# An attention block's row maxima transposed in SBUF, and two down projections of each block held for the next

## The chip, the cores and the metric

The kernel is one program on one NeuronCore of a Trainium2 chip. Its time is the device time in microseconds of one execution. Five engines run side by side, each through its own list of instructions in order: PE (TensorE, matrix products into PSUM), DVE (VectorE), ACT (ScalarE), POOL (GpSimd, which here works on SBUF only) and SP, whose list holds the DMA issues. PEld in a profile is PE's weight load, which can lie beside its matmuls. Engines wait for each other by semaphores.

## The reference

Shapes: one sequence of 2048 rows of width 512; 32 query heads of 16 columns share one key and one value head; a gated feed-forward of width 1792.

```python
mod = (silu(c) @ w_mod)                     # sa, ca, ga, sb, cb, gb: rows of 512
h = layernorm(x) * (1 + ca) + sa
q, k, v = h @ wq, h @ wk, h @ wv            # q: 32 heads of 16; k, v: one head of 16
p = softmax(q k^T / 4)                      # per head, over 2048 keys
x = x + ga * ((p v, heads side by side) @ wo)
h = layernorm(x) * (1 + cb) + sb
x = x + gb * (((h @ w_gate) * (h @ w_up)) @ w_down)
```

All in float32. The kernel splits operands of most products into a float16 high part and a float16 low part, and adds three products for one (terms high-high, low-high, high-low); p v is done in float32.

## The kernel before, in words

The sequence is cut into NB = 4 blocks of 512 rows, and each block's 32 heads into 8 groups of four: 32 units u = 8 b + g. A unit takes 32 **steps**; step s = 32 u + i. A step does one key tile for half of the unit: `qk_exp` makes two score tiles of 128x512 (L487, tile sc) which ACT exponentiates into P (L600), and `pv` multiplies earlier P tiles with the values (L612). There are 1024 steps and 2048 exponentials, so two exponentials in a trace are one step.

The exponent needs the maximum of each row of scores first. It is found by a second, earlier pass over the same scores: `max_mm` makes a 128x512 tile (L487, tile mx) and DVE reduces it to one column (L564, mpart). This pass runs LEAD = 38 steps ahead of the main one, two reduces a step; the first 38 steps of it are a loop of their own (the lead), in which PE also does the first layer norm's transposes, K, V and some of Q. When a unit's 32 maximum steps are done, `max_fin` reduces mpart to mm (128 rows x 16 numbers, L570), and two steps later `max_rows` turns mm into rows: PE transposes it into a PSUM tile mxt that is taken from the two buffers of tag "mx" (L576), ACT writes the float16 high part (L581), DVE the low part (L582), and SP sends the two to rows 48 and 49 (and 112 and 113) of the unit's query tile sst (L585). These rows ride along in the score product and subtract the maximum, so they must have landed when the unit's first score product starts.

Everything else of PE is **fill**: `fill` is a list of groups of matmuls, each with a due step. A group is emitted in pairs: one pair is two halves of four 64x32 tiles (8 matmul instructions, tile misc), which fill the PE array once. `pace` spreads what is left evenly over the steps to the due step, and `fill_gap` gives a step 0 to BURST = 3 pairs. A block's fill is made one block later: at step i = 16 of the first unit of block b, the work of block b-1 is queued: four groups of the output projection (`wo_work`, 12 pairs each), the transposes of the second layer norm (`ln2_work`, four single pieces, the first at least TR_GAP = 8 steps after the groups before it), 28 groups of gate and up (12 pairs), and four down projections (42 pairs each, two by two). That is 48 + 336 + 168 = 552 pairs. The due step is 12 steps into the next block. For the last block in the loop (b = 3) the due step is the loop's end, and RESERVE keeps the four down projections of block 2 out of the loop: they, and the whole feed-forward of block 3, are done after it with full 128x128 tiles (L520).

POOL makes the float16 parts of weights, queries, layer-norm rows and gated products; in the first half of the program it also prepares all weights (`late_weights`, tile wsl), one piece every 2.5 steps. x1 is a row tile after attention: it lives from its output projection (L701) until its down projection has been added (L812), and is taken from four buffers of tag "x1".

Two lines set where the fill of a step ends and how a unit's maxima are handed over:

```python
n = min(int(credit[0]), BURST)                       # fill_gap, L1139
for gap, it in zip((TR_GAP, 0, 0, 0), ln):           # L1267, layer norm transposes
later[mstep[0] + 1] = (f, g)                         # max_half, L1039
```

Of the kernel before, what the change touches and what calls it, by code (L numbers as in the profile page):

```python
# [13 lines left out]
F32 = mybir.dt.float32  # L14
# [10 lines left out]
NU = NB * UB  # L25
KT = S // 128
FT = F // 128
LEAD = 38
ABS_GAP = 2.5
SPLIT_GAP = 2.5  # L30
NSC = 2
# [7 lines left out]
SWAP_WAIT = 2  # L39
EV_WAIT = 1  # L40
TURN = 12
RESERVE = 31000.0
TR_GAP = 8
BURST = 3
# [11 lines left out]
def adaln_mqa_glu_kernel(ctx: ExitStack, tc: tile.TileContext, x_in, wq_in, wk_in, wv_in, wo_in,  # L56
# [204 lines left out]
                             start=(k == 0), stop=(k == KC - 1))  # L261

    def split_rows(dst, p, scale, mscale, bias):
        hi = work.tile([128, BT], F16, name="hi", tag="x1", bufs=4)
        nc.scalar.activation(hi, p, AF.Identity, bias=bias, scale=mscale)
        nc.vector.scalar_tensor_tensor(dst, p, scale, hi, op0=OP.mult, op1=OP.subtract)

# [300 lines left out]
    def max_fin(u):  # L568
        mms[u] = work.tile([128, 2, 8], F32, name="mm")
        nc.vector.tensor_reduce(mms[u], mparts[u].rearrange("p a q t k -> p a (q t) k"), axis=AX.X, op=OP.max)  # L570

    def max_rows(u):
        def f():
            p = psum.tile([16, 128], F32, name="mxt", tag="mx", bufs=NMX)
            mms[u, "p"] = p
            nc.tensor.transpose(p, mms[u].rearrange("p a c -> p (a c)"), ident)  # L576

        def g():
            p = mms[u, "p"]
            mt = [work.tile([16, 128], F16, name=f"mt{hl}") for hl in range(2)]  # L580
            nc.scalar.activation(mt[0], p, AF.Copy, scale=1.0 / 32.0)  # L581
            nc.vector.scalar_tensor_tensor(mt[1], p, 1.0 / 32.0, mt[0], op0=OP.mult, op1=OP.subtract)  # L582
            s = sst[u % 3]
            for hl in range(2):
                nc.sync.dma_start(s[48 + hl:113 + hl:64, :, :], mt[hl])  # L585
        return [(100, f, g)]

    pvb = {}
# [92 lines left out]
    def wo_work(b):  # L681
        def op(t):
            def f(i):
                ch, term = divmod(i, 3)
                ol, wl = TERMS[term]
                return och[b, ch][:, ol, t * 128:(t + 1) * 128], wo[:, wl, ch, :]
            return f

        def pre(t):
            def f(tag=None):  # L690
                load_x(b, t)
                return ps_misc(tag=tag)
            return f

        def fin(t):
            def f(p):
                if b < NB - 1:
                    x1 = work.tile([128, D], F32, name="x1", tag="x1", bufs=4)
                else:
                    x1 = work.tile([128, D], F32, name="x1p", tag="P", bufs=NP)  # L700
                nc.vector.scalar_tensor_tensor(x1, p, sca[:, 7:8], xls[b, t], op0=OP.mult, op1=OP.add)  # L701
                x1s[b, t] = x1
                s2 = work.tile([128, 1, 2], F32, name="st2", bufs=5)
                bs = work.tile([128, 6], F32, name="bs", bufs=4)
                nb = work.tile([128, 2], F32, name="nb", bufs=4)
                yt = {}

                def spread():
                    nc.vector.bn_stats(bs, x1)

                def aggr():
                    nc.vector.bn_aggr(s2[:, 0, :], bs)
                    yt["y"] = rstd_of(s2, 1)
                    nc.gpsimd.tensor_tensor(nb[:, 0:1], s2[:, 0, 0:1], yt["y"], op=OP.mult)
                    nc.gpsimd.tensor_scalar(nb[:, 1:2], nb[:, 0:1], -1.0, 0.0, op0=OP.mult, op1=OP.add)

                def nrm():
                    n2 = work.tile([128, D], F32, name="n2", tag="och", bufs=4)
                    nc.scalar.activation(n2, x1, AF.Identity, bias=nb[:, 1:2], scale=yt["y"])
                    n2s[b, t] = n2  # L720

                after(2, spread)
                after(3 + t % 2, aggr)
                n2f[b, t] = nrm
                if t == 3:
                    for j, d in enumerate((2, 3, 5, 7)):
                        after(d, n2f[b, j])
            return f

        return [Group(3 * KC, op(t), pre(t), fin(t)) for t in range(4)]  # L730
# [107 lines left out]
    def late_weights():  # L838
# [19 lines left out]
            nc.sync.dma_start(md, st["row"][64:128:32, :])  # L858
            st["md"] = md

        gab = work.tile([128, D], F32, name="gab", tag="x1", bufs=4)
        gbb = consts.tile([128, D], F32, name="gbb")

        def m3():
# [189 lines left out]
    def seg_left():  # L1054
        n = sum(2 * x.g.n - x.k for x in live())
        return n / 2.0
# [77 lines left out]
    def fill_gap(step):  # L1134
        if cur["segs"] is None and not plan(step):
            return
        if step < cur["wait"]:
            return
        n = min(int(credit[0]), BURST)  # L1139
        late = -(-seg_left() // max(NU * NSTEP - 8 - step, 1))  # L1140
        burst_turn(step, max(1, n, int(late)))

# [79 lines left out]
        return [(g,) for two in gu for g in two] + twos(down)  # L1222

    early["on"] = False
    for u in range(NU):
        b, g = divmod(u, UB)
        if u == 1:
            side.extend(dlist)
        for i in range(NSTEP):
# [31 lines left out]
            if i == 16 and u > 0 and g == 0:  # L1261
# [2 lines left out]
                gate = [step + 4, 0]  # L1264
                for gr in wo_work(b - 1):
                    fill.append((gate, "prod", (gr,), due))
                for gap, it in zip((TR_GAP, 0, 0, 0), ln):  # L1267
                    fill.append(([None, gap], "solo", it, due))
                gate = [None, 0]
                for gs in ffn_twos(b - 1):  # L1270
                    fill.append((gate, "prod", gs, due))

    def drain_all():
# [66 lines left out]
```

## Time and profile before

| | |
|---|---|
| runs shown | 1734.56, 1729.01, 1734.06 us; median 1734.06 |
| profiled execution | 1740.9 us, span of instructions 1739.1 us |
| mean granted PE clock | 0.993 |
| PE, DVE, ACT, POOL busy | 1686.9, 1406.3, 1253.0, 560.1 us |
| first exponential of step 0 | 92.8 us after the span's start |
| work after the loop | from about 1574 us to the end |

To read it: an engine's busy share over the whole span mixes stages with different limits. Here the stage of a step matters: how many pairs of fill it was given, and whether the maxima are still being made. The stretches of the program that the prediction uses are bounded by the starts of the steps' first exponentials: step 272 (454.0 us), 320 (534.4), 512 (826.3), 528 (851.1), 592 (947.7), 752 (1189.4), 784 (1238.8), 848 (1333.5), 976 (1513.8).

### The profile page before, as it was taken

Reading aid. Unit: us, or ns where it says so; the run is one execution under the profiler, and the core shown is the slowest. Engines: PE = TensorE matmul, PEld = TensorE weight load, DVE = VectorE, ACT = ScalarE, POOL = GpSimd, SP = SyncE. Lnnn points to the kernel's source line nnn. Section 1 sums busy time; section 2 is a strip of 40 time slices with the busy share of each in tenths; the row PEclk is TensorE's granted clock in tenths of the full one; section 3 lists DMA queues with packets and bytes.
Section 4 is the critical chain, followed back from the end, with each engine's and each line's share of the span. In section 5 each row is a group of like instructions: output and inputs, shape, how many; then the busy total and the mean of one; then the engine's idle time right before and its main releaser. Section 6 shows DMA issues by size and latency. Waiting matters only on the chain. (4 is left out here: it accounts for less than half of the span.)

```text
span 1739.1 us, 102797 instructions
## 1 busy us (share of the span) xinstructions
PE 1686.9 (97%) x47395; PEld 972.1 (56%) x47395; DVE 1406.3 (81%) x2353; ACT 1253.0 (72%) x2319; POOL 560.1 (32%) x745
## 2 busy tenths in 40 slices
PE   6899999999999999999999999999999999999999
PEld 3345555544546566566556666666556666654444
DVE  7899999999987888888898888888999999912110
ACT  3479898989876787777787777777788888883110
POOL 5824444637575842210022212210021222221130
PEclk9999999999998999999999999999999999999999
DMA  5212232312322210000100000000100000001000
GB/s 198 102 33 82 63 88 62 93 40 86 84 70 58 66 28 17 7 17 25 43 24 19 13 19 13 8 19 21 49 17 19 12 19 13 15 7 46 15 1 25
DMA packets 49180, 71.10 MB, mean 41 GB/s; under 512 B 15270, under 2 KB 29418, under 8 KB 48748
## 3 DMA queue, kind: packets, MB, share of 16 engines
q1 hardware_dynamic: 47164, 64.33, 12.3%
q8 instruction: 370, 6.06, 1.5%
q14 instruction: 62, 0.51, 0.1%
q10 hardware_dynamic: 1584, 0.20, 0.1%
HBM read 51.12 MB, written 8.92 MB: 35 GB/s over the span
## 5 line engine op out<-in xcount | busy, mean ns | idle before, releaser
L564 DVE TENSOR_REDUCE mpart<-mx 128x1 f32<-128x512 f32 x2048 | 1290.8, 683 | 125.1 <-PE mx L487 110.5
L600 ACT ACTIVATE P<-sc 128x512 f32<-128x512 f32 x2048 | 1128.4, 599 | 279.6 <-PE sc L487 235.9
L612 PE MATMUL pv<-P,vst 64*32 64x256 f32 x16384 | 1172.3, 383 | 0.3 <-issue 0.3
L487 PE MATMUL mx<-kst,sst 48*32 48x512 f16 x8192 | 819.8, 382 | 25.9 <-DVE mpart L564 19.2
L487 PE MATMUL sc<-sst,kst 50*32 50x512 f16 x8192 | 828.8, 379 | 2.3 <-ACT P L600 2.0
L487 PEld LDWEIGHTS <-sst 48*32 48x32 f16 x8192 | 333.2, 91 | 355.7 <-issue 243.0
L612 PEld LDWEIGHTS pv<-P,vst 64*32 64x32 f32 x16384 | 418.2, 105 | 56.5 <-issue 5.3
L487 PEld LDWEIGHTS <-kst 50*32 50x32 f16 x8192 | 303.3, 91 | 75.7 <-issue 32.8
L487 PE MATMUL misc<-h2T,wg 64*32 64x512 f16 x4032 | 307.1, 379 | 0.3
L487 PE MATMUL misc<-h2T,wu 64*32 64x512 f16 x4032 | 305.1, 376 | 0.7 <-issue 0.2
L795 POOL TENSOR_TENSOR gf<-gf,g 128x512 f32<-128x512 f32 x42 | 53.9, 1282 | 470.8 <-ACT gf L794 470.6
L487 PEld LDWEIGHTS <-wu 64*32 64x32 f16 x4032 | 111.1, 92 | 40.1 <-issue 12.9
L487 PEld LDWEIGHTS <-wg 64*32 64x32 f16 x4032 | 112.4, 93 | 37.8 <-issue 13.5
L487 PE MATMUL misc<-wd,glu 64*32 64x512 f16 x2688 | 114.1, 376 | 0.1
L787 ACT ACTIVATE g<-misc 128x512 f32<-128x512 f32 x56 | 33.6, 601 | 75.8 <-PE misc L520 75.5
L652 POOL TENSOR_TENSOR oc<-oc,rr 128x512 f32<-128x512 f32 x15 | 19.3, 1285 | 213.7 <-DMA rr<-ri 186.2
L487 PE MATMUL misc<-h,wq 64*32 64x512 f16 x1536 | 85.0, 378 | 0.6
L520 PE MATMUL misc<-wd,glu 128*128 128x512 f16 x336 | 73.2, 379 | 0.0
L487 PEld LDWEIGHTS <-glu 64*32 64x32 f16 x2688 | 53.1, 93 | 26.1 <-issue 6.0
L799 POOL TENSOR_TENSOR glu<-gf,glu 128x512 f16<-128x512 f32 x56 | 65.1, 1163 | 4.7
L797 DVE TENSOR_TENSOR gf<-misc,g 128x512 f32<-128x512 f32 x14 | 9.7, 692 | 62.9 <-PE misc L520 62.9
L625 DVE SCALAR_TENSOR_TENSOR ev<-pv,evs,ev 128x512 f32<-128x512 f32 x32 | 23.8, 743 | 45.1 <-ACT ev L620 36.4
(231 smaller groups left out, 1037.3 us busy)
## 6 DMA issues: line engine op xcount, KB each, us to landing
wsl<-in_B_w_gate_dram SPq DMA_DIRECT2D x32, 224.0 KB
wsl<-in_B_w_up_dram SPq DMA_DIRECT2D x32, 224.0 KB
wsl<-in_B_w_down_dram SPq DMA_DIRECT2D x28, 256.0 KB
sst<-qd SPq DMA_DIRECT2D x186, 32.0 KB
qd<-q SPq DMA_DIRECT2D x16, 256.0 KB
oc<-ev SPq DMA_DIRECT2D x128, 32.0 KB
rr<-ri SPq DMA_DIRECT2D x16, 256.0 KB
xl<-in_A_x_dram SPq DMA_DIRECT2D x16, 256.0 KB
```

The costliest lines, as they stand in the source:

```text
L487: return [nc.tensor.matmul(p[c:c + CW, :], left[:, c:c + CW], right, start=start, stop=stop) for c in range(0, 128, CW)]
L520: nc.tensor.matmul(p, left, right, start=i == 0, stop=i == g.n - 1)
L564: nc.vector.tensor_reduce(mparts[u][:, a, p, t, kc:kc + 1], m, axis=AX.X, op=OP.max)
L600: nc.scalar.activation(ptl[u, kt, a][:, p, :], t, AF.Exp)
L612: nc.tensor.matmul(pvb[u, r][32 * j:32 * j + 32, c * w:(c + 1) * w], vst[ks, kt, :], ptl[u, kt, a][ks, p, c * w:(c + 1) * w], start=(kt == ...
L625: nc.vector.scalar_tensor_tensor(ev, pvb[u, 1], evs, ev, op0=OP.mult, op1=OP.add)
L652: eng.tensor_tensor(o, o, st["r"], op=OP.mult)
L787: nc.scalar.activation(st["g", f], p, AF.Copy, scale=2.0 ** -45)
L795: nc.gpsimd.tensor_tensor(gf, gf, st["g", f], op=OP.mult)
L797: nc.vector.tensor_tensor(gf, p, st["g", f], op=OP.mult)
L799: nc.gpsimd.tensor_tensor(st["glu"][:, 1, f, :], gf, st["glu"][:, 0, f, :], op=OP.subtract)
```

## The change

Four things change. LEAD goes from 38 to 40. The maxima are split into float16 parts by POOL, before they are transposed: three small POOL instructions in `max_fin`; `max_rows` is one DVE transpose in SBUF, in blocks of 32x32, and eight DMAs of 16 runs of 64 bytes in place of two of 16 runs of 256. The last two down projections of a block (one item of two groups, 84 pairs) are taken from the list of blocks 0 and 1 and queued in the next block, between the output projection and the layer norm's transposes, whose gap of eight steps then goes to zero; for that, x1 has six buffers. And a burst that would leave a single last pair of a turn takes it along, or leaves two.

```diff
-LEAD = 38
+LEAD = 40
...
+NX1 = 6
+HELD_DUE = 44
...
-        hi = work.tile([128, BT], F16, name="hi", tag="x1", bufs=4)
+        hi = work.tile([128, BT], F16, name="hi", tag="x1", bufs=NX1)
...
     def max_fin(u):
         mms[u] = work.tile([128, 2, 8], F32, name="mm")
         nc.vector.tensor_reduce(mms[u], mparts[u].rearrange("p a q t k -> p a (q t) k"), axis=AX.X, op=OP.max)
+        mm = mms[u]
+        hl = mms[u, "hl"] = work.tile([128, 2, 2, 8], F16, name="mhl")
+        nc.gpsimd.tensor_scalar(mm, mm, 1.0 / 32.0, 0.0, op0=OP.mult, op1=OP.add)
+        nc.gpsimd.tensor_scalar(hl[:, 0], mm, 1.0, 0.0, op0=OP.mult, op1=OP.add)
+        nc.gpsimd.tensor_tensor(hl[:, 1], mm, hl[:, 0], op=OP.subtract)
 
     def max_rows(u):
         def f():
-            p = psum.tile([16, 128], F32, name="mxt", tag="mx", bufs=NMX)
-            mms[u, "p"] = p
-            nc.tensor.transpose(p, mms[u].rearrange("p a c -> p (a c)"), ident)
+            mt = mms[u, "t"] = work.tile([128, 32], F16, name="mt")
+            nc.vector.transpose(mt, mms[u, "hl"].rearrange("p l a c -> p (l a c)"))
 
         def g():
-            p = mms[u, "p"]
-            mt = [work.tile([16, 128], F16, name=f"mt{hl}") for hl in range(2)]
-            nc.scalar.activation(mt[0], p, AF.Copy, scale=1.0 / 32.0)
-            nc.vector.scalar_tensor_tensor(mt[1], p, 1.0 / 32.0, mt[0], op0=OP.mult, op1=OP.subtract)
-            s = sst[u % 3]
             for hl in range(2):
-                nc.sync.dma_start(s[48 + hl:113 + hl:64, :, :], mt[hl])
+                rows = sst[u % 3][48 + hl:113 + hl:64, :, :].rearrange("a p (t j r) -> a p t j r", j=4, r=32)
+                for j in range(4):
+                    nc.sync.dma_start(rows[:, :, :, j, :], mms[u, "t"][32 * j + 16 * hl:32 * j + 16 * hl + 16, :])
         return [(100, f, g)]
...
         n = min(int(credit[0]), BURST)
+        left = max(x[2] - x[1] for x in cur["segs"] if x) - cur["j"]
+        if left - n == 1:
+            n += 1 if n < BURST else -1
         late = -(-seg_left() // max(NU * NSTEP - 8 - step, 1))
...
+                for gs in held:
+                    fill.append((gate, "prod", gs, step + HELD_DUE))
-                for gap, it in zip((TR_GAP, 0, 0, 0), ln):
+                for gap, it in zip((0 if held else TR_GAP, 0, 0, 0), ln):
                     fill.append(([None, gap], "solo", it, due))
                 gate = [None, 0]
-                for gs in ffn_twos(b - 1):
+                work_items = ffn_twos(b - 1)
+                held = [work_items.pop()] if b < NB - 1 else []
+                for gs in work_items:
                     fill.append((gate, "prod", gs, due))
```

(The two other x1 tiles take NX1 buffers too, and `held` starts as an empty list ahead of the loop. Lines after the first added one move down by two to eight: L564 is L566 in the changed kernel, L812 is L815.)

The order that results is shown at three places. First DVE's list where the maxima of a unit in block 0 are handed over; mpart is the column of a reduced tile, mt the transposed rows. Before:

```order
L564 TENSOR_REDUCE mpart<-mx 128x1 x46
L570 TENSOR_REDUCE mm<-mpart 128x16
L564 TENSOR_REDUCE mpart<-mx 128x1 x4
L582 SCALAR_TENSOR_TENSOR mt_6434<-mxt,mt_6433 16x128
L564 TENSOR_REDUCE mpart<-mx 128x1 x14
L625 SCALAR_TENSOR_TENSOR ev<-pv,evs,ev 128x512
```

and in the changed kernel:

```order
L566 TENSOR_REDUCE mpart<-mx 128x1 x42
L572 TENSOR_REDUCE mm<-mpart 128x16
L566 TENSOR_REDUCE mpart<-mx 128x1 x4
L582 STREAM_TRANSPOSE mt<-mhl 128x32
L566 TENSOR_REDUCE mpart<-mx 128x1 x18
L628 SCALAR_TENSOR_TENSOR ev<-pv,evs,ev 128x512
```

Four reduces still stand between mm and the transposed rows, and the hand-over has moved four reduces (two steps) away from ev, the previous unit's end.

Second, SP's list around the same hand-over; sst is the query tile, qd the stored queries, wsl a slice of weights. Before:

```order
L551 DMA sst_122<-qd_2_2367 16x2x512 x6
L874 DMA wsl<-in_B_w_up_dram 128x448 x4
L585 DMA sst_120<-mt_6433 2x8x128
L585 DMA sst_120<-mt_6434 2x8x128
L874 DMA wsl<-in_B_w_up_dram 128x448
```

and in the changed kernel:

```order
L553 DMA sst_122<-qd_2_2329 16x2x512 x6
L877 DMA wsl<-in_B_w_up_dram 128x448 x4
L588 DMA sst_120<-mt 2x8x32 x8
L877 DMA wsl<-in_B_w_up_dram 128x448
L536 DMA qd_0_6547<-q_6542 128x1024
```

Two issues have become eight at one place of the list; their neighbours are the same.

Third, DVE's list after the output projection of block 1, up to the next hand-over of maxima but one (L701 and L704 end an output projection, L812 and L815 a down projection). Before, the last two down projections of block 0 stand far ahead of this place:

```order
L701 SCALAR_TENSOR_TENSOR x_27421<-misc,sca,xl 128x512
L564 TENSOR_REDUCE mpart<-mx 128x1 x2
L709 BN_STATS bs<-x_27421 128x6
L564 TENSOR_REDUCE mpart<-mx 128x1 x4
L712 BN_AGGR st_27423<-bs 128x2
L564 TENSOR_REDUCE mpart<-mx 128x1 x20
L570 TENSOR_REDUCE mm<-mpart 128x16
```

and in the changed kernel one of them follows here, and the other ten reduces later:

```order
L704 SCALAR_TENSOR_TENSOR x_26792<-misc,sca,xl 128x512
L566 TENSOR_REDUCE mpart<-mx 128x1 x2
L712 BN_STATS bs<-x_26792 128x6
L566 TENSOR_REDUCE mpart<-mx 128x1 x4
L715 BN_AGGR st_26794<-bs 128x2
L566 TENSOR_REDUCE mpart<-mx 128x1 x24
L572 TENSOR_REDUCE mm<-mpart 128x16
L566 TENSOR_REDUCE mpart<-mx 128x1 x4
L582 STREAM_TRANSPOSE mt<-mhl 128x32
L566 TENSOR_REDUCE mpart<-mx 128x1 x16
L815 SCALAR_TENSOR_TENSOR x_13780<-misc,sca,x_13780 128x512
```

In steps: the output projection of block 1 now ends at step 552 (556 before), the two held down projections are made in steps 549 to 582, and the layer norm's transposes stand at steps 583, 584, 585 and 587 (565 to 568 before). Of the 80 steps from 512 to 591 there are 22 without a pair of fill before, and 16 after. What is left for the work after the loop is the same in both: four down projections of block 2 and all of block 3.

More of the change, by code (lines that the diff above doesn't have):

```diff
@@ L697, in f @@
                 if b < NB - 1:
-                    x1 = work.tile([128, D], F32, name="x1", tag="x1", bufs=4)
+                    x1 = work.tile([128, D], F32, name="x1", tag="x1", bufs=NX1)
                 else:
@@ L859, in m2 @@
             st["md"] = md
-        gab = work.tile([128, D], F32, name="gab", tag="x1", bufs=4)
+        gab = work.tile([128, D], F32, name="gab", tag="x1", bufs=NX1)
         gbb = consts.tile([128, D], F32, name="gbb")
@@ L1224, in adaln_mqa_glu_kernel @@
     early["on"] = False
+    held = []
     for u in range(NU):
```

## The prediction

> **What bounds the kernel now.** I read the page first, then DVE's and PE's timelines, then stretches by step, then the waits.
>
> ```profile
> span 1739.1 us, 102797 instructions
> PE 1686.9 (97%) x47395; PEld 972.1 (56%) x47395; DVE 1406.3 (81%) x2353; ACT 1253.0 (72%) x2319; POOL 560.1 (32%) x745
> 299.86 0.68 DVE L564 TENSOR_REDUCE mpart<-mx 128x1 f32<-128x512 f32 x1
> 300.93 0.28 DVE L582 SCALAR_TENSOR_TENSOR mt<-mxt,mt 16x128 f16<-16x128 f32 x1 [0.39 <-ACT mt L581]
> 301.14 8.79 DVE L564 TENSOR_REDUCE mpart<-mx 128x1 f32<-128x512 f32 x14
> 310.51 18.39 DVE L564 TENSOR_REDUCE mpart<-mx 128x1 f32<-128x512 f32 x30
> 1610.44 124.77 PE misc L520 x578
> ```
>
> PE at 97% looks like the only bound, but that is occupancy by tiles that need not fill the array. In block 0 DVE's reduces follow each other every 18.39/30 = 0.613 us, so a step of two reduces cannot be shorter than 1.23 us. A full 128x512 matmul of the tail takes 124.77/578 = 0.216 us, and one pair of fill (8 instructions) occupies the array for as long. To see what a step costs where fill is plentiful, I count exponentials (two are a step) and misc matmuls in two stretches.
>
> ```profile
> 947.70:1189.40 241.70, 174.89 (x320) 1.00 0.07 16
> 1333.50:1513.80 180.30, 140.26 (x257) 1.00 0.06 14
> 947.70:1189.40 241.70, 122.60 (x3104) 0.00 (x0) 1.49 (x2) 15.02 (x25) 1.00 0.07 16
> 1333.50:1513.80 180.30, 82.37 (x1960) 0.00 (x0) 0.00 (x0) 12.04 (x20) 1.00 0.06 14
> ```
>
> The first two rows are the exponentials: 160 steps of 1.511 us, 128 steps of 1.409. The last two are misc: 388 pairs, 2.43 a step, and 245 pairs, 1.91 a step. The slope between them is 0.20 us a pair, close to the 0.216 of a full matmul, and both leave 0.99 us for a step without fill. So a step takes the larger of 1.23 us (DVE) and 0.99 + 0.216 x pairs (PE). With two pairs or more PE is the bound and every pair costs its full time; with none, 0.24 us of PE goes unused. The block borders are such places: 826.3 to 947.7 and 1189.4 to 1333.5 us, steps 512 to 591 and 752 to 847.
>
> ```profile
> 826.30:947.70 121.40, 47.56 (x1024) 1.68 (x16) 4.48 (x6) 5.15 (x7) 1.00 0.11 30
> 1189.40:1333.50 144.10, 56.39 (x1208) 1.67 (x16) 4.47 (x6) 4.55 (x6) 1.00 0.09 26
> 454.00:534.40 80.40, 26.24 (x448) 1.68 (x16) 2.98 (x4) 3.26 (x4) 0.92 0.26 72
> 851.10:923.40 72.30, 23.74 (x448) 1.68 (x16) 2.98 (x4) 3.35 (x4) 1.00 0.10 27
> 515.30:518.70 3.40, 1.85 (x46) 0.73 (x45) 2.32 (x5) 1.46 (x3) 3.23 (x5) 1.00 0.25 72
> 518.70:532.40 13.70, 13.38 (x209) 6.84 (x212) 6.51 (x10) 6.62 (x13) 11.95 (x16) 0.50 0.19 53
> 517.70 0.78 ACT L751 ACTIVATE hf<-misc,hsc 128x512 f32<-128x512 f32 x1 [1.95 <-POOL h2T L754]
> ```
>
> Border 1 to 2: 80 steps and (1024-16)/8 = 126 pairs, 79.2 + 27.2 = 106.4 us by the rule, 121.4 measured: 15.0 us of slack. Border 2 to 3: 96 steps, 149 pairs, 127.2 against 144.1: 16.9. Border 0 to 1 (third row) has the same 448 misc matmuls in its 48 steps as the fourth row, yet takes 8.1 us longer. There ACT waited 1.95 us for POOL, PE was busy 1.85 of 3.40 us, and then the granted clock was 0.50 for 13.7 us, which alone is worth 6.8.
>
> **The change part by part.** *Maxima off PE.* In block 0 the hand-over costs DVE the time from 300.54 (the reduce's end) to 301.14: 0.60 us. Elsewhere it costs PE:
>
> ```profile
> 674.00 0.40 PE L487 MATMUL sc<-sst,kst 50*32 50x512 f16 x4
> 674.51 0.28 PE L576 MATMUL mxt<-ident,mm 128*16 128x128 f32 x1
> 674.72 0.40 PE L487 MATMUL misc<-h2T,wu 64*32 64x512 f16 x4
> PEld mxt L576 <- DVE mpart L564: 16.1, 31, 0.8
> DVE mt L582 <- ACT mt L581: 14.1, 30, 3.1
> L570 DVE TENSOR_REDUCE mm<-mpart 128x16 f32<-128x64 f32 x32 | 7.0, 220 | 1.1
> L712 DVE BATCH_NORM_AGGREGATE st<-bs 128x2 f32<-128x6 f32 x16 | 2.8, 173 | 0.1
> L715 POOL TENSOR_SCALAR nb<-nb 128x1 f32<-128x1 f32 x16 | 3.1, 192 | 1.4
> ```
>
> Score tiles lie 0.216 us apart, so the array was free from about 674.22 and takes up full work again at 674.72: 0.50 us. Removed per unit: PE's transpose with its wait, ACT's 0.25 us, DVE's 0.28 with its wait, and one of two mx buffers being held meanwhile. Added: one DVE transpose (no row; between 0.17, the small aggregate, and 0.28, the instruction it replaces; I take 0.20, near the small 220 ns reduce), and three POOL instructions of 16 columns at 0.2 to 0.3 us, 0.85 us together. DVE's transpose stands four reduces (2.45 us) behind mm, so it waits only if POOL is over 1.6 us late. The 8 hand-overs of DVE-bound steps (units 1 to 8) give 0.60 - 0.20 = 0.4 each, 3.2 us; the 23 in PE-bound steps about 0.43 of the 0.50, 9.9 us, since DVE has slack there. Together **-13 us** (bounds -16 and -6: DVE gives nothing back, or the PE hole is filled by the fill's own waits). The Trainium skill, VectorE: DVE Perf Modes, "The three transpose paths", gives 311 ns for a 128x128 bf16 transpose in 32x32 blocks; a quarter of that would be an estimate of 0.08 us, 1 us less in the sum; no run shows it yet.
>
> *SP.* Eight issues in place of two.
>
> ```profile
> L585 SPq DMA_DIRECT2D sst<-mt x64: 503/544/597, 86.0 to 1531.4; - x64
> 300.92 1.53 SPq L585 DMA_DIRECT2D sst<-mt  x2
> 92.80:306.70 213.90, 179.33 (x320) 0.99 0.22 63
> SPq L647 <- DMA ri<-rc: 28.6, 16, 2.7
> ```
>
> At 0.65 us an issue with its gap, six more are 3.9 us. The rows start 2 steps (2.5 us) earlier, and the path PE 0.28, ACT 0.25, DVE 0.28 shrinks to 0.2. So the last issue ends some 0.8 us later against the unit's first use: 303.3 for the unit whose first exponential starts at 306.7 (320 exponentials, five units, lie before it). PE needs the rows about 0.6 us ahead of that; a small DMA lands within 28.6/16 = 1.8 us. That leaves 1.0 us. Cost **0**, up to +4 if issues of 64-byte runs are a fifth slower. Behind them on SP stand weight slices, which POOL does not need at once.
>
> *LEAD.* Two more lead steps of two reduces, which have no main step beside them.
>
> ```profile
> 75.82 6.35 DVE L564 TENSOR_REDUCE mpart<-mx 128x1 f32<-128x512 f32 x10
> ```
>
> Four reduces at 0.635 are 2.5 us; at the end two steps are without maxima, 0.43 us of PE. **+2** (0 to +4: PE's clock is at half before and after this place already).
>
> *Held down projections.* All fill is PE work that is done anyway; only slack counts. Of 80 steps at border 1 to 2, 16 instead of 22 have no pair: 6 x 0.24 = 1.4 us. The rest of the gain is the layer norm: 4 x 0.75 (x1) and 4 x 0.68 (statistics) on DVE and 4 x 0.81 on ACT, 9 us, now stand in steps of 3 pairs, 1.64 us long, where DVE and ACT have 0.4 us to spare; I take 3 us of it. The four transposes stay exposed. So 4.5 us a border, **-9** for two (bounds -16, all slack but the transposes gone, and 0, rival 1).
>
> *Border 0 to 1.* No held work there, but the transposes move: steps 310, 311, 312, 314 in place of 309 to 312, and POOL's list has one weight slice moved ahead of the first h2T. The buffer for which ACT waited 1.95 us is then free by the time. If PE has no hole, the half clock does not come: **-8**. The Trainium skill, TensorE: Matmul & The Clock Gate, Part 1, says the clock is halved after an idle window of some 3.4 us and released after a busy one. The trace agrees with the first (the window ahead of the fall was 1.85 busy of 3.40) and shows 13.7 us, four windows, until the release; by the rule the fall goes with the hole.
>
> *Single last pairs.* In block 0 some twelve times 2 and 0 pairs in place of 1 and 1: a step of two costs 1.42 instead of 1.23, mostly absorbed by the two mx buffers: **+1**.
>
> Sum: -13 + 0 + 2 - 9 - 8 + 1 = -27 us. From the profiled 1740.9 that is 1714. The runs' median, 1734.06, is 6.8 below the profiled execution, just what the half clock cost there; I read the ordinary runs as having less of it, so from them I take -20: 1734 - 20 = **1714** too.
>
> **The rivals.** (1) *Held work gains nothing.* PE is 97% busy, and the slack of the borders may be waits of turns and evacuations that come with any fill. For: only 7.1 of the 15.0 us at border 1 to 2 are explained by fill-free steps (22 x 0.24 = 5.3) and by sixteen transposes, which the tail has in one row:
>
> ```profile
> 1608.69 1.75 PE misc L744 x16
> ```
>
> Against: the 0.4 us a step of room. 1714 + 9 = 1723. (2) *The clock falls all the same*, at border 0 to 1 or behind the two longer lead steps, where PE does little: 1714 + 7 = 1721. (3) *SP is the wait*: issues of 0.9 us instead of 0.65 make the rows 1.0 us late in 8 units and scarcely late where a step is 1.4 us or longer: +8, 1722; at 1.5 us an issue (+6.8) they would be late in all. (4) *Slower: DVE waits for POOL.* DVE's list is in order; a transpose that waits stops all reduces, then PE by its two mx buffers. POOL's gate-and-up group is
>
> ```profile
> L795 POOL TENSOR_TENSOR gf<-gf,g 128x512 f32<-128x512 f32 x42 | 53.9, 1282 | 470.8 <-ACT gf L794 470.6
> L798 POOL TENSOR_SCALAR glu<-gf 128x512 f16<-128x512 f32 x56 | 34.8, 621 | 72.3 <-DVE gf L797 68.7
> L799 POOL TENSOR_TENSOR glu<-gf,glu 128x512 f16<-128x512 f32 x56 | 65.1, 1163 | 4.7
> ```
>
> 3.07 us long; if the maxima stood behind a whole one in every unit, DVE would lose 1.5 us each, 46 us: 1760. Break-even with the gain of 20 is at 14 of 31 units. Against: POOL itself waited 470.6 us for ACT ahead of L795, so it is seldom behind, and the work that stands ahead of the three instructions in the new order had ended before mm in all units but one of this execution.
>
> **How the numbers follow.** Forecast 0.52 (1706 to 1719); rival 1 0.17; rival 2 0.14; rival 3 0.09; rival 4 0.05; something unseen 0.03. What this kernel's timing can tell from no change is about 0.3%, 5.2 us: faster means below 1728.9. The forecast and rivals 1 to 3 lie there but for their upper edges, where two of them come together: faster 0.87, same 0.08, slower 0.05. Range: lower edge 1703 (all bounds of maxima and held work good), upper 1726 (two rivals at once).
>
> **What would show it.** Right: no wait of DVE's transpose on POOL over 0.2 us; no hole on PE two steps behind mm; step 320 less than 76 us behind step 272 with a clock of 1.00; steps 512 to 591 with 34 pairs more (160) in about 123 us instead of 121.4; the middle of blocks 1 and 2 at about 1.42 and 1.45 us a step. Wrong: PE waiting for a DMA into sst at a unit's start (rival 3), DVE waiting for POOL's mhl (rival 4), a clock of 0.5 in a new place (rival 2), a border stretch longer by 7 us (rival 1).

## The result, and the profile after

The changed kernel takes 1716.08 us, the median of 5 runs (1711.3 to 1723.72), against 1734.56 for the kernel before in the same comparison (5 runs, 1729.01 to 1738.43): a ratio of 0.9896, 95% interval 0.986 to 0.9932. The forecast was 1714, in a range of 1703 to 1726. The profiled executions are 1723.72 us (span 1721.7) now and 1740.9 (span 1739.1) before, so the two traces differ by 17.2 us. Ratios leave out executions over 1.5% longer than the fastest of the same kernel.

The head of the page, then the groups by line of the new hand-over of the maxima (busy us, mean ns of one, idle time before it and what ended it):

```profile
span 1721.7 us, 103076 instructions
PE 1668.7 (97%) x47363; PEld 989.8 (57%) x47363; DVE 1404.9 (82%) x2353; ACT 1252.2 (73%) x2287; POOL 578.6 (34%) x841
```

```profile
L577 POOL TENSOR_TENSOR mhl<-mm,mhl 128x16 f16<-128x16 f32 x32 | 7.0, 218 | 2.7
...
L575 POOL TENSOR_SCALAR mm<-mm 128x16 f32<-128x16 f32 x32 | 6.5, 203 | 234.2 <-DVE mm L572 225.7 <-DVE sct L937 8.1
L576 POOL TENSOR_SCALAR mhl<-mm 128x16 f16<-128x16 f32 x32 | 6.5, 203 | 2.6
L582 DVE STREAM_TRANSPOSE mt<-mhl 128x32 f16<-128x32 f16 x32 | 6.5, 202 | 0.9 <-POOL mhl L577 0.9
```

The transpose takes 202 ns, where 0.20 us had been taken, and POOL's three instructions 203 to 218 each. POOL stands ready and waits for DVE (225.7 us in all), and DVE waited for POOL once in 32 units, 0.9 us. Next the waits (us in total, times, longest), first one of the kernel before, then those of the changed kernel, and SyncE's issues of one unit:

```profile
PEld pv L612 <- issue: 5.3, 21, 0.4
```

```profile
PEld pv L615 <- issue: 13.5, 34, 1.2
...
PE sc L489 <- DMA sst<-mt: 1.1, 1, 1.1
```

```profile
941.82 4.34 SPq L588 DMA_DIRECT2D sst<-mt  x8
```

PE's 31 waits for the maxima's transpose (16.1 us before) are gone, and it waits once for the new rows. What has grown is "issue", time in which an engine waited for nothing that the profile shows: ahead of the weight loads of the P x V products it goes from 5.3 us in 21 times to 13.5 in 34. The stretches by step follow, exponentials first (two a step), then the misc matmuls:

```profile
454.80:526.30 71.50, 52.60 (x96) 1.00 0.26 76
526.30:804.10 277.80, 209.92 (x384) 0.99 0.12 31
804.10:927.60 123.50, 88.08 (x161) 1.00 0.12 34
927.60:1158.30 230.70, 174.69 (x321) 1.00 0.06 15
1158.30:1308.50 150.20, 105.79 (x193) 1.00 0.10 29
1308.50:1496.90 188.40, 140.69 (x256) 1.00 0.06 14
```

```profile
804.10:927.60 123.50, 57.64 (x1300) 1.68 (x16) 6.00 (x8) 3.11 (x4) 1.00 0.12 34
...
1158.30:1308.50 150.20, 71.66 (x1600) 1.68 (x16) 6.01 (x8) 3.11 (x4) 1.00 0.10 29
```

Border 0 to 1 (first row) has a granted clock of 1.00 and takes 71.5 us instead of 80.4. Border 1 to 2 takes 123.5 instead of 121.4, with (1300 - 16)/8 = 160.5 pairs instead of 126. Border 2 to 3 takes 150.2 instead of 144.1 with 198 pairs instead of 149. By the rule of 0.99 + 0.216 x pairs a step, the slack fell from 15.0 to 9.6 us and from 16.9 to 12.4. The two stretches between the borders (the fourth and the sixth row) take 1.442 and 1.472 us a step, where 1.42 and 1.45 had been put down as a sign of being right.

Worked out from the first exponential of steps 0, 272, 320 and 1008 of each trace (us; the names of the later columns are those of the experiments):

```
                  before  LEAD 40  maxima+  held  no pair  changed  changed,
                          only     LEAD 40  only  rule              LEAD 38
to step 0           92.8    97.2     96.7   93.5    96.3     94.8     92.8
steps 0-271        361.2   363.7    358.0  361.4   358.1    360.0    371.1
steps 272-319       80.4    75.8     74.9   71.4    70.7     71.6     77.1
steps 320-1007    1023.4  1025.1   1020.9 1016.1  1016.4   1014.3   1009.6
from step 1008     181.3   183.1    181.2  181.2   181.2    181.1    181.2
span              1739.1  1745.1   1731.7 1723.5  1722.7   1721.7   1731.8
```

In the changed kernel the half of the gain that had been put on PE-bound steps is missing: -9.0 (21 hand-overs) and -9 (held work) had been forecast for steps 320 to 1007, and -9.1 came.

### The profile page after: what moved, and what is told of

It reads as the page before. It is cut to its first block, busy times and chain, and to the rows that moved or that the text cites. A ratio compares the mean times of both kernels' runs of the same rounds, so it can differ in the third digit from the quotient of the medians.

```text
span 1721.7 us, 103076 instructions
## 1 busy us (share of the span) xinstructions
PE 1668.7 (97%) x47363; PEld 989.8 (57%) x47363; DVE 1404.9 (82%) x2353; ACT 1252.2 (73%) x2287; POOL 578.6 (34%) x841
## 4 chain that ended last, share of the span: by engine, by line
PE 86%; DVE 9%; issue 2%; DMA 1%; ACT 1%; POOL 1%; SPq 0%; DVEq 0%; ACTq 0%; POOLq 0%
PE pv L615 23%; PE misc L489 22%; PE mx L489 18%; PE sc L489 13%; PE misc L522 9%; DVE mpart L566 7%; DMA wmA<-in_w_mod_dram 1%; ACT P L603 1%; DVE ev L628 1%; PE misc L747 0%; PE misc L262 0%; PE pv L452 0%; POOL h L405 0%; PE pv L262 0%; PE misc L849 0%
## 5 line engine op out<-in xcount | busy, mean ns | idle before, releaser
L566 DVE TENSOR_REDUCE mpart<-mx 128x1 f32<-128x512 f32 x2048 | 1294.2, 684 | 117.9 <-PE mx L489 100.8
L615 PEld LDWEIGHTS pv<-P,vst 64*32 64x32 f32 x16384 | 424.7, 105 | 65.8 <-issue 13.5
L489 PEld LDWEIGHTS <-kst 50*32 50x32 f16 x8192 | 309.4, 90 | 82.3 <-issue 40.6
L489 PE MATMUL misc<-h2T,wg 64*32 64x512 f16 x4032 | 314.4, 377 | 2.4 <-issue 2.1
L489 PE MATMUL misc<-h2T,wu 64*32 64x512 f16 x4032 | 313.2, 377 | 0.9 <-issue 0.4
L489 PEld LDWEIGHTS <-wg 64*32 64x32 f16 x4032 | 117.3, 92 | 38.3 <-issue 16.1
L489 PEld LDWEIGHTS <-wu 64*32 64x32 f16 x4032 | 116.2, 92 | 36.0 <-issue 14.3
L489 PE MATMUL misc<-wd,glu 64*32 64x512 f16 x2688 | 123.2, 376 | 0.7 <-issue 0.6
L575 POOL TENSOR_SCALAR mm<-mm 128x16 f32<-128x16 f32 x32 | 6.5, 203 | 234.2 <-DVE mm L572 225.7
L489 PEld LDWEIGHTS <-glu 64*32 64x32 f16 x2688 | 59.1, 93 | 24.3 <-issue 5.5
```

What stands on the lines that cost most here:

```text
L489: return [nc.tensor.matmul(p[c:c + CW, :], left[:, c:c + CW], right, start=start, stop=stop) for c in range(0, 128, CW)]
L566: nc.vector.tensor_reduce(mparts[u][:, a, p, t, kc:kc + 1], m, axis=AX.X, op=OP.max)
L575: nc.gpsimd.tensor_scalar(mm, mm, 1.0 / 32.0, 0.0, op0=OP.mult, op1=OP.add)
L615: nc.tensor.matmul(pvb[u, r][32 * j:32 * j + 32, c * w:(c + 1) * w], vst[ks, kt, :], ptl[u, kt, a][ks, p, c * w:(c + 1) * w], start=(kt == ...
```

## The experiments: the parts alone

The kernel before had medians of 1733.7 to 1739.1 us from one comparison to the next, so every kernel is set against the runs of before that stood beside it; ratios have 95% intervals.

**The new hand-over with LEAD 40, and LEAD 40 alone.** The first is the kernel before with these lines, the second with only the first of them:

```diff
-LEAD = 38
+LEAD = 40
+        nc.gpsimd.tensor_scalar(mm, mm, 1.0 / 32.0, 0.0, op0=OP.mult, op1=OP.add)
...
-            nc.tensor.transpose(p, mms[u].rearrange("p a c -> p (a c)"), ident)
+            nc.vector.transpose(mt, mms[u, "hl"].rearrange("p l a c -> p (l a c)"))
...
-                nc.sync.dma_start(s[48 + hl:113 + hl:64, :, :], mt[hl])
+                for j in range(4):
+                    nc.sync.dma_start(rows[:, :, :, j, :], ...)
```

> The kernel before with the new hand-over of the maxima (POOL's split, DVE's transpose, eight DMAs) and LEAD 40; down projections, x1 buffers and turns as before. Theory (the terms maxima -13 and LEAD +2): about -11 us, 1723; in the stretches by step, 320 to 512 and 592 to 752 shorter by 0.43 us a unit (2.6 and 2.2 us), block 0 by 0.4 a unit. Border 0 to 1 (steps 272 to 320) stays at about 80 us with its stretch at half clock, since the fill there is as before. Rival A (the PE hole of a hand-over is refilled by fill that waits anyway, so only block 0 gains): -3.2 + 2 = about -1 us, 1733. Rival B (the new hand-over alone gains all that the change gained): -18, 1716.

> The kernel before with LEAD 40 in place of 38, nothing else. Theory (the term LEAD +2): 1734 + 2 = 1736, of it 2.0 to 2.5 us ahead of the first main step, and 0.4 us back at the end. Rival 2 (the longer lead lets the clock fall behind it for longer): the stretch of half clock behind the lead lasts 3.4 us longer, +1.7 more, 1738, and this cost then belongs to LEAD. Rival C (a lead of 40 lets the unit's maxima and rows come two steps earlier everywhere and gains by itself): 1728 or less.

Hand-over and LEAD: 1736.3 us against 1739.12, ratio 0.9989 (0.9973 to 1.0004), which can't be told from the kernel before. LEAD alone: 1744.64, ratio 1.0028 (1.0013 to 1.0043). So the hand-over by itself is worth 8.3 us and not 13, and LEAD alone costs 5.5 and not 2. In the hand-over's own step nothing is wrong. It stands 27 steps into a unit, with LEAD 40 it stands 25; the time over the rule there was 0.59 us on the mean of block 0 and 0.41 in units 10 to 30, and is 0.05 and -0.03 now. But over steps 320 to 1007 the two kernels with LEAD 40 differ by 1025.1 - 1020.9 = 4.2 us, where 21 hand-overs at 0.43 make 9.0. Something in those steps takes back half. In block 0 the term was met: steps 32 to 271 take 3.6 us less with the new hand-over (312.8 against 316.4, both with LEAD 40), where eight times 0.4 are 3.2. In the trace of LEAD alone the way to step 0 is 4.4 us longer and steps 0 to 31 another 2.8 (47.3 us against 44.5). Half clock behind the lead lasts 10.2 us there instead of 3.4, and another 3.4 us of it lie inside the lead. And DVE, in the old hand-over, came to wait longer for ACT (14.1 us before), with PE behind it:

```profile
DVE mt L582 <- ACT mt L581: 19.5, 31, 2.8
...
PE mx L487 <- DVE mt L582: 4.1, 6, 0.9
```

**Held projections alone.** The changed kernel with the old hand-over, LEAD 38 and no rule for last pairs:

```diff
-LEAD = 40
+LEAD = 38
...
-        left = max(x[2] - x[1] for x in cur["segs"] if x) - cur["j"]
-        if left - n == 1:
-            n += 1 if n < BURST else -1
```

> The changed kernel with the old hand-over of the maxima, LEAD 38 and no rule for single last pairs: only the held down projections and the six x1 buffers are left. Theory (the terms held -9 and border 0 to 1 -8, the latter counting only if the half clock is gone there): about -17 us against the profiled execution of the kernel before, -10 to -13 against the median, 1721 to 1724; steps 512 to 592 at about 123 us with 34 pairs more, steps 592 to 752 about 8 us shorter. Rival 1 (held work gains nothing): 512 to 592 grows by 34 x 0.216 = 7 us to 128, and the total is within 3 us of the kernel before, 1731 to 1737. Rival 2 (the clock falls all the same at border 0 to 1): steps 272 to 320 take 78 us or more.

1728.83 us against 1739.12, ratio 0.9943 (0.9925 to 0.9961): 10.3 us. Steps 320 to 1007 are 7.3 us shorter. Rival 1 is out: steps 512 to 591 take 125.5 us with 160.5 pairs, not 128, and their slack is 11.6 instead of 15.0; the slack of border 2 to 3 goes from 16.9 to 9.8; between the borders it grows by some 3 us. At border 0 to 1 there is no half clock (71.4 us). With the old fill it takes 80.4, 75.8 and 74.9 us in the three traces, with 13.7, 3.4 and 3.4 us at half clock; with the new fill 71.4, 70.7 and 71.6 with none (a fourth kernel with the new fill, the last of this section, has half clock there for another reason). So the term of -8 is right for the profiled execution, and some 4 us of it hold against the two other traces with the old fill.

**Without the rule for single last pairs.** The changed kernel less the three lines just shown:

> The changed kernel without its rule for single last pairs (1 and 1 pairs in place of 2 and 0). Theory (the term single last pairs +1): 1716 - 1 = 1715, which is not to be told from the changed kernel. Rival (the rule is what moved the fill at border 0 to 1 and took the half clock away): steps 272 to 320 go back to about 80 us with a clock of 0.5 in them, 1716 + 7 = 1723. Rival (the rule makes the 2.0 us hole and the half clock at 641.9 us in the changed kernel): that stretch of half clock is gone, 1716 - 4 = 1712.

1722.02 us, ratio 0.9899 (0.9881 to 0.9917), the changed kernel's 0.9896: the rule does nothing that can be measured. Border 0 to 1 is free of half clock without it, so it isn't what cured it. This kernel holds the other parts together: 17.1 us below the kernel before, where hand-over with LEAD and held work alone gave 2.8 and 10.3, 13.1 in sum. The 4 us between lie inside the intervals, some 3 us for each of the three.

**The changed kernel with LEAD 38.**

```diff
-LEAD = 40
+LEAD = 38
```

> The changed kernel with LEAD 38 in place of 40. Theory (the term LEAD +2, two lead steps of two reduces): 2 us below the changed kernel, that is 20 us below the kernel before. Rival C (LEAD alone measured +5.5 us on the kernel before, so the two steps cost as much here): 23 to 24 us below. Rival 3 (SP: the rows come 2.5 us later against their first use, and the margin behind eight issues was 1 to 3 us): PE waits for the DMA into sst at more than two units' starts, and the kernel is not faster than the changed one.

1733.94 us against 1737.05, ratio 0.9982 (0.9968 to 0.9996): not 20 us below the kernel before but 3. Rival 3 describes it. In block 0 the last step ahead of a unit's first scores is 1.56 us over the rule on the mean of units 1 to 7 (0.02 in the kernel before, 0.34 in the changed one), steps 0 to 271 take 371.1 instead of 360.0 us, and PE waits for the rows:

```profile
PE sc L489 <- DMA sst<-mt: 10.7, 8, 3.6
...
PEld L489 <- DMA sst<-mt: 3.7, 3, 2.2
```

This is the margin that the prediction had put at 1.0 us for LEAD 40: two steps less, 2.5 us, make it -1.5. So eight issues cost nothing only because LEAD 40 covers them, and the 2 us of LEAD are the price of that cover. In steps 320 to 1007, where steps are longer, the kernel is no slower for it (1009.6 us against 1014.3 with LEAD 40).

Rival 4 shows here too. Border 0 to 1 takes 77.1 us, with 3.4 us of half clock, though its fill is the new one: DVE's transpose waits for POOL, the reduces wait behind it, and PE stands for 2.06 us ahead of 534.03. Of the waits between 524 and 543 us:

```profile
DVE mt L582 <- POOL mhl L577: 2.0, 1, 2.0
PE mx L489 <- DVE mpart L566: 1.7, 1, 1.7
```

## The experiments: what takes the gain back in PE-bound steps

**What the traces show.** PE's instructions are moved by DMA while the kernel runs. The rows of the DMA queues (packets, MB, share of 16 engines), of the kernel before and of the changed one:

```profile
q8 instruction: 370, 6.06, 1.5%
```

```profile
q8 instruction: 371, 6.08, 1.5%
```

94,790 matmul and weight-load records over 370 packets of 16 KB are 256 a packet. In steps 320 to 1007 packets stand 3.9 us apart on the mean; a transfer takes 0.9 to 1.6 us, and the next one never begins sooner than 2.2 us behind its end (2.7 in the middle). I counted, between 530 and 1560 us, every start on PE more than 0.2 us behind the one before it that has no semaphore to wait for and stands at the start of a packet (that is at every 256th of PE's records), and what these gaps have above 0.216 us, the normal distance:

```
kernel                        stops    us    above 0.216
before                          28    10.6       4.6
LEAD 40 only                    29    11.2       4.9
held only                       30    11.1       4.7
maxima + LEAD 40                45    18.3       8.6
changed, LEAD 38                48    21.4      11.0
changed, no pair rule           59    26.3      13.6
changed                         54    26.8      15.2
```

Of the changed kernel's 54 gaps over 0.3 us without a wait in these stretches, wherever they stand, 44 are at a packet's first instruction (of the rest, six lie in a stretch of half clock), of the kernel before's 24, 21; they end 1.2 to 1.6 us behind the end of the packet's transfer. The reading that the next experiments test is that PE stops there because it has no instructions: the holes of the old hand-overs gave the supply time to catch up, and without them PE gets to the end of what it has. By this reading, without the 10.6 us by which the stops grew, the -9.1 of steps 320 to 1007 would have been -19.7, close to the 18 forecast. Two of the changed kernel's stops are long, 2.08 us at 549.8 and 2.28 at 643.9; the packets that end them began 5.9 and 6.0 us behind the ones before, and why isn't shown. The second brought a new fall of the clock. One of the longer stops of the kernel before, the second long one of the changed kernel (PE's weight loads), then all engines by stretch (PE, PEld, DVE, ACT, POOL, clock, DMA):

```profile
802.24 0.09 PEld L487 LDWEIGHTS <-kst 50*32 50x32 f16 x1 [0.63 <-issue]
```

```profile
641.56 0.10 PEld L489 LDWEIGHTS <-kst 50*32 50x32 f16 x3
643.94 0.10 PEld L489 LDWEIGHTS <-sst 48*32 48x32 f16 x4 [2.28 <-issue]
```

```profile
641.00:644.50 3.50, 1.60 (x64) 0.96 (x56) 1.65 (x4) 1.59 (x3) 2.18 (x3) 1.00 0.16 44
644.50:647.90 3.40, 3.40 (x80) 1.98 (x68) 1.96 (x3) 1.79 (x3) 0.86 (x1) 0.50 0.02 5
647.90:651.30 3.40, 3.40 (x132) 2.36 (x115) 2.96 (x5) 2.51 (x5) 0.00 (x0) 0.99 0.02 5
```

PE was busy 1.60 of 3.50 us, then ran at half clock for 3.4 us, worth 1.7. The prediction quoted the Trainium skill, TensorE: Matmul & The Clock Gate, Part 1, on a release after one busy window of some 3.4 us; this stretch agrees, and the 13.7 us of the kernel before, in which PE was busy for 13.38, did not. The prediction also took the other half of the Trainium skill's rule, a fall behind an idle window, as borne out; but the windows ahead of the two falls were no idle ones, PE was busy for 1.85 of 3.40 us and for 1.60 of 3.50.

**Wider tiles: fewer instructions for the same products.**

```diff
-CW = 32
+CW = 64
```

CW is the number of columns of a score, maximum or fill tile. The next three kernels are the changed one with CW 64 and 128, and the kernel before with 64.

> The changed kernel with CW 64 in place of 32: score, maximum and fill matmuls are issued as two tiles of 64 columns in place of four of 32, same products, half as many of these PE instructions. Theory S (new, from the traces: PE's matmul and weight-load instructions come in packets of 16 KB, 256 instructions, each transfer begins at least 2.2 us behind the end of the one before, and PE stops, without any wait, only at each 256th instruction until some 1.4 us behind a packet's end; such stops over 0.3 us add up to 9.8 us in steps 320 to 1023 of the kernel before and to 27.6 us in the changed one, and so took back what the maxima gave): the stops are gone, 27.6 less 54 x 0.216 = 16 us below the changed kernel, 30 to 36 below the kernel before. Rival (the stops are not supply, or wider tiles overlap less on the array): stops stay, or the time is that of the changed kernel or above, -18 to +20 us against the kernel before.

> The changed kernel with CW 128: one matmul of 64 rows and 128 columns in place of four of 32 columns, same products. Theory S: no stop for want of instructions either, and the same time as with CW 64 within 3 us, since the array's work is the same. Rival (a tile of 128 columns shuts out the four 32-column tiles that run beside it): each step longer by up to 0.2 us, slower than the kernel before by 100 us or more.

> The kernel before with CW 64. Theory S: its stops over 0.3 us, 24 in steps 320 to 1023, 9.8 less 24 x 0.216 = 4.6 us, are gone, and nothing else changes: about 5 us below the kernel before; against it the changed kernel with CW 64 then stands 28 to 30 us lower, since the removed hand-overs are paid in full (terms maxima -13, held -9, border 0 to 1 up to -8, LEAD +2 to +5). Rival (supply has no part in it): changed and before differ by 18 us with CW 64 too.

4687.53 us (ratio 2.697), 4626.24 (2.662) and 4713.44 (2.712): all three far off, and no test of the theory, since something larger took over. Busy time of the engines and the granted clock in 40 slices, then PE's timeline, of the changed kernel with CW 64; last, for comparison, two rows of the changed kernel itself:

```profile
PE 4658.9 (99%) x32451; PEld 1061.4 (23%) x32451; DVE 1532.3 (33%) x2353; ACT 1370.3 (29%) x2287; POOL 577.3 (12%) x841
...
PEclk8555555555555555555555555555555555555569
```

```profile
999.65 0.64 PE L489 MATMUL mx<-kst,sst 48*64 48x512 f16 x2
1000.22 1.08 PE L615 MATMUL pv<-P,vst 64*32 64x256 f32 x8
1001.23 0.64 PE L489 MATMUL sc<-sst,kst 50*64 50x512 f16 x2
```

```profile
1000.52 0.40 PE L489 MATMUL mx<-kst,sst 48*32 48x512 f16 x4
1000.55 0.40 PE L615 MATMUL pv<-P,vst 64*32 64x256 f32 x4
```

The 32-column tiles of P x V no longer run beside the others (0.03 us behind mx in the changed kernel) but after them, and the clock stays at 0.5 from 95 us to the end of the loop at 4520, though PE shows work 99% of the time. The Trainium skill, TensorEngine Tiling (Array Packing), under Tiling Modes, says that a change of the tiling mode drains TensorE; this timeline agrees with it. Why the clock stays low isn't settled: the Trainium skill, TensorE: Matmul & The Clock Gate, Part 1, ties the clock to how busy PE has been and expects full rate after a busy window, which this run doesn't show.

**Half the P x V instructions, same tiles.** PARTS is the number of pieces of a P x V product. With one piece the whole product stands where its first half stood, ahead of the step's second maximum tile:

```diff
-PARTS = 2
+PARTS = 1
...
-            pv(*who, 1)
```

> The changed kernel with PARTS 1: each P x V product of a step is issued as four matmuls of 512 columns in place of eight of 256, same tiles of 64 rows and 32 columns, same products, 16,384 matmuls and weight loads fewer of 94,800 on PE. Theory S (PE stops at packet boundaries for want of instructions): packets fall from 371 to about 306, their mean distance in the main steps grows from 3.9 to about 4.6 us, the stops without a wait at a 256th instruction vanish, and the kernel is 12 to 18 us below the changed one, 30 to 36 below the kernel before. Rival (the stops are an effect of something else, the array is the bound): within 4 us of the changed kernel, 14 to 22 below the kernel before. Rival (a P x V matmul of twice the length holds up the tiles behind it): slower than the changed kernel.

> The kernel before with PARTS 1, nothing else. Theory S: it had only 24 such stops, 4.6 us over the normal distance, so about 5 us below the kernel before, 1732; the difference between changed and before then widens from 18 us to about 29. Rival: the same difference of 18 us as with eight matmuls.

> The kernel before with the new hand-over of the maxima, LEAD 40 and PARTS 1. With eight P x V matmuls this hand-over and LEAD 40 together measured -2.8 us where the terms -13 and +2 had said -11. Theory S: the rest went into stops for instructions (15.4 us of them against 9.8), so here the terms hold: 10 to 13 us below the kernel before with PARTS 1, about 15 below the kernel before. Rival A (a hand-over's hole in PE-bound steps is filled by other waits anyway): 3 us below the kernel before with PARTS 1.

The changed kernel: 1820.52 us, ratio 1.0501 (1.0486 to 1.0515). The kernel before: 1851.59, 1.0683 (1.0669 to 1.0698). The kernel before with the new hand-over and LEAD 40: 1835.73, 1.0588 (1.0574 to 1.0603). In absolute time all three missed, and the first text's second rival describes what came: with PARTS 1 a step is some 0.1 us longer, also in block 0, more than the stops were worth. Whether the longer matmuls do that or the new place of the second half, these runs don't separate. But the stops are gone, and the three can be compared with each other. The packets of the changed kernel with PARTS 1:

```profile
q8 instruction: 307, 5.03, 1.1%
```

By the count above they have 0 stops (changed), 1 (maxima) and 3 (before), 0.2 us above the normal distance at most, with packets 4.9 to 5.0 us apart on the mean of steps 320 to 1007. And now the parts pay in full. The hand-over with LEAD 40 brings 1851.59 - 1835.73 = 15.9 us (10 to 13 had been expected, 2.8 were measured with eight matmuls), of it 1097.7 - 1087.2 = 10.5 in steps 320 to 1007, where the term says 9.0. The hole of the old hand-over is no longer than before: its steps, 26 to 28 of a unit, together stand 0.52 us above the line that the other steps give (time against pairs, units 10 to 30), and 0.50 with eight matmuls. The whole change brings 31.1 us instead of 18.5. That fits the theory; since these steps are also longer for another reason, and the whole change brings more than the 29 expected, it doesn't prove it alone.

**Late instructions on purpose.** The changed kernel with a copy that nothing reads:

```diff
+    extra = dram.tile([1536, D], F32, name="extra")
...
+        if 10 <= u <= 30:
+            nc.sync.dma_start(extra, x_rows[0:1536, :])
```

> The changed kernel with an extra copy of 3 MB from device memory to device memory, which nothing reads, behind the load of each unit's q rows for units 10 to 30: it takes no compute engine and keeps the 16 DMA engines busy for an estimated 15 to 20 us a unit. Theory S (PE stops at packet boundaries because the next packet of 256 instructions is not there): instruction packets that move beside the copy take 1.4 us or more instead of 0.9 to 1.1, some four to five a unit, 80 to 100 in all, each up to 0.5 us later; the stops without a wait at a 256th instruction grow from 27 us by 10 to 45 us, and the time with them, 1726 to 1760; block 0, where no copy runs and PE has time to spare, is unchanged. Rival (the stops have nothing to do with the packets): the time within 4 us of the changed kernel, and the stops as many as before, unless PE is seen to wait for a load by name.

1831.25 us, the median of six (1811.24 to 1847.6), against 1738.19, ratio 1.0477 (1.0434 to 1.052), 100 to 110 us above the changed kernel: the sign of the theory, and far more than its 10 to 45. The profiled execution is the longest of the six. PE's timeline over one copy, and the stretches of all engines around it:

```profile
672.21 0.40 PE L489 MATMUL misc<-h2T,wu 64*32 64x512 f16 x4
672.25 0.40 PE L489 MATMUL misc<-h2T,wg 64*32 64x512 f16 x4
677.28 0.61 PE L489 MATMUL mx<-kst,sst 48*32 48x512 f16 x4 [4.64 <-issue]
```

```profile
672.00:677.40 5.40, 0.76 (x32) 0.27 (x24) 0.78 (x2) 0.94 (x2) 0.00 (x0) 0.84 0.72 258
677.40:682.00 4.60, 4.60 (x94) 2.28 (x97) 2.67 (x4) 2.54 (x5) 1.14 (x1) 0.50 0.02 4
```

With the DMA engines 72% busy, PE stands for 4.6 us without a wait, all other engines run dry behind it, and the clock falls. The stops at packet starts now have 88.0 us above the normal distance instead of 15.2, and half clock lasts 126 us instead of 17, worth 55 more: together 128, where the spans of the two profiled executions differ by 124. Block 0, without a copy, is unchanged (358.7 and 360.0 us). One part of the theory was wrong: the packets aren't slower (1.10 us on the mean in both), they begin late. A copy takes 9 us of the 16 engines, not 15 to 20. Behind each of the 21 copies one packet begins 6.6 to 10.8 us after the one before it, and PE stops for 1.1 to 5.8 us at a packet start. No wait of PE for a named load came with the copy but one of 0.4 us. So packets of instructions that are late make PE stop at packet starts, and that is shown; that the stops also took back the missing half of the gain rests on the count and on the PARTS kernels.

## Why the prediction was right, and where it was not

The time is 2.1 us above the forecast, but not every step held: of the 27 us forecast against the profiled execution 17.2 came, while the 20 taken from the median, 7 less for half clock, were nearly met (18.5). That near hit is in part luck. The 7 us were taken off because the profiled execution of the kernel before was 6.8 us above its median, put down to half clock at border 0 to 1; that of the changed kernel, without half clock there, is 7.6 above its own. So the deduction stood against the 9 us missing in the PE-bound steps, and only the profiled executions have a trace.

- **Maxima off PE, -13: mechanism right, size wrong in PE-bound steps.** 8.3 us with LEAD held equal. Block 0 gave its part (3.6 us), and each hole of 0.43 us is gone; but of the 9.0 us of steps 320 to 1007 4.2 are left, while stops at packet starts rise from 4.9 to 8.6 us above the normal distance, which is 3.7 of the missing 4.8. The step that failed is "PE is the bound and every pair costs its full time": PE's bound had a second part, its supply, that the row of the instruction queue showed and no rival named. The transpose at 202 ns is as taken; an estimate of 0.08 us, a quarter of the Trainium skill's 311 ns in VectorE: DVE Perf Modes, "The three transpose paths", is not what the runs show.
- **SP, 0: nearly right**, by its margin. With LEAD 40 there is one wait of 1.1 us, and in block 0 the steps ahead of a unit's first scores are 0.3 us longer than before, some 2 us in seven units; with LEAD 38 the computed -1.5 us came as 1.56. The eight issues take 4.34 us, 0.54 each, below the 0.65 taken.
- **LEAD, +2: too small, and wrong as a separate term.** The way to step 0 grew by 2.0 us in this trace, but by 3.5 to 4.4 in the three other traces with LEAD 40 in the table. On the old hand-over it costs 5.5, and under the new one leaving it out costs 15: its price and SP's zero are one edit.
- **Held, -9: about right.** -10.3 alone, with border 0 to 1 in it; -7.3 in steps 320 to 1007.
- **Border 0 to 1, -8: right against the profiled execution** (-8.8), about half against other traces. The cause named, the wait of ACT for a buffer of POOL's, is gone with the new fill; a wait of 2.0 us of DVE for POOL brings half clock back with LEAD 38.
- **Single last pairs, +1: nothing** that can be measured (0.9899 against 0.9896).
- **Rivals.** (1) fell with the held projections alone. (2) came in part: in the changed kernel's trace none at border 0 to 1, 3.4 us more behind the lead, which it had named, and 3.4 us behind the stop that ends at 643.9, a place that nobody named. (3) is real at LEAD 38. (4) had no weight in the changed kernel (0.9 us in 32 units); in the traces of three other kernels with the new hand-over it is 1.8 to 3.6 us.

No kernel of these beats the changed one; without the pair rule it is as fast.

## What to carry to other kernels

Where an engine shows nearly full time, ask what its instructions need beside its array: divide the records by the packets of its instruction queue, and look whether stops without a wait fall on packet starts. Here, removing a small wait from such an engine paid in full only where the supply was ahead. And two edits of which one is the cover of the other (here eight issues and two lead steps) want one price, tried together and apart.

## What the runs showed of the hardware that was not expected

- PE's instructions come 256 at a time. In the changed kernel ten packets in a row stood 3.58 us apart on the mean at the closest (steps 320 to 1007); beside a copy that kept the DMA engines 72% busy the next packet came late and PE stood for 4.6 us.
- Tiles of 64 or 128 columns mixed with tiles of 32 ran one after the other, and the clock stayed at 0.5 with PE at 99%.
- A stretch of half clock lasted 3.4, 6.8, 10.2 or 13.7 us, multiples of about 3.4. In seven traces (the table of stretches) the six falls of the clock between 110 and 1580 us came behind a hole on PE of 1.5 to 2.6 us; two more holes, of 1.92 and 2.08 us, brought none.
